# Attention blocks in pairs, and TensorE in source order, in a fused attention and expert kernel

## Chip, cores, metric

One Trainium2 chip, one of its cores. The metric is the device time of one execution in microseconds (us), lower is better. PE is TensorE, DVE is VectorE, ACT is ScalarE, POOL is GpSimd, SP the engine whose queue issues most of the DMAs.

## What is computed

Windowed attention, a dense layer with a clipped square as activation, then a routed layer with eight experts, of which each token takes one:

```python
scores = where(0 <= i - j < 64, q @ k.T / sqrt(64), -1e9)      # 4 x 8 heads, 576 tokens, 64 wide
attn   = exp(scores - max); attn /= sum + 1e-9
x = (attn @ v).transpose(0, 2, 1, 3).reshape(2304, 512)
h = x @ w_in                                                   # 512 x 2048
g = where(h >= 1, h, where(h <= -1, 0, (h + 1)**2 / 4))
x = g @ w_out                                                  # 2048 x 512
logits = x @ w_gate + modality_bias[modality_id]               # 8 experts
out[token] = gate * (relu(x @ w1[e]) @ w2[e]),  e = argmax(logits)
```

## The kernel before

The 2304 tokens are worked in six chunks of 384 (`NC`, `CT`). An attention block is 64 tokens with their eight heads, so a chunk has six blocks (`BPC`). While the dense layer runs for chunk c, the attention blocks of chunk c+1 are put between its steps. A chunk has 16 steps, f = 0 to 15, one for each 128 columns of the hidden layer. In a step PE does the first layer for f (`l1`, L435) and the second layer for f-2 (`l2`, L469, with `LAG` = 2). From chunk 1 on both layers work on a high and a low part of each operand (`gh` and `gl` from `gsplit`, L459): 12 matmuls for the first layer, and nine for the second, three for each of its three token tiles, the third of these on the low part. In chunk 0 both layers run in plain fp32, and DVE and ACT decode the weights beside that, one pair of tiles in a step (`dec_abs` on ACT, `dec_clamp` and `dec_merge` on DVE).

An attention block passes through five stages. `att_mm` (L321) makes scores on PE, `att_max` (L335) masks them and takes the maxima on DVE, `att_exp` (L350) takes exponentials and row sums on ACT. `att_norm` (L361) inverts the sums on DVE and scales, on ACT for the blocks of chunk 1 and on POOL later. `att_tr` (L380) transposes on PE, with a copy on ACT. `att_pv` (L393) multiplies by v in 16 matmul instructions of 64 output columns, two for each of the eight heads, and `att_x` (L412) copies the result out on ACT and leaves its low part on DVE. Scores, transposes, products with v and the rank products of the router share three PSUM banks (`aux`, L93).

Before, a new block starts at every second step. In chunk 0 (`step0`, L951) block number BPC + k starts at step `FIRST[k]`, is normalised one step later, transposed three and multiplied by v four steps later. In chunks 1 to 4 the loop over `its` (L995) starts it at `S0[k]`, transposes two and multiplies four steps later.

Who orders the instructions: in chunk 0 PE, DVE, ACT and POOL run in the order in which the source issues them (`manual_schedule`, `m0`). With chunk 1 this ends (`m0.close()`, L1005), and a planner with a model of the engines' times orders each engine's queue anew, except SP, which is in source order throughout. PE comes back to source order in the last part (L1075). A queue, once ordered, runs strictly in that order: what stands behind a waiting instruction waits too.

From step 1 of a chunk on the router of the chunk before runs as a generator (`route`, L514), one piece a step: it copies the second layer's results, makes the logits on DVE (L536), a one-hot of the chosen expert (L556), and at step 9 the rank products on PE (L561 and L563), in the source between the first and the second layer of that step.

Of the kernel before, what the change touches and what calls it, by code (L numbers as in the profile page):

```python
# [70 lines left out]
def moe_kernel(ctx, tc, qT, kT, v, w_in, w_out, mod, wg, wgT, mbias, w1, w2, cst, tri, empty, out, spec):  # L71
# [289 lines left out]
    def att_norm(i):  # L361
        att_sum(i)
        att_scale(i)
# [28 lines left out]

    def att_pv(i):  # L393
        ts = at.pop(i)
        vt = vs.pop(i)
        w = window(i)[0]
        if i < BPC:
            xo = ps.tile([P, KD, BLK], F32, name=f"xo{i}", tag="h", bufs=2)
        else:
            xo = aux([P, KD, BLK], f"xo{i}")  # L400
        for hp in range(KD):
            for a in range(2):
                T.matmul(
                    xo[a * D : (a + 1) * D, hp, :],
                    vt[:w, (2 * hp + a) * D : (2 * hp + a + 1) * D],
                    ts[:w, hp, a * BLK : (a + 1) * BLK],
                    start=True,
                    stop=True,
                )
        xos[i] = xo  # L410

    def att_x(i):  # L412
        xo = xos.pop(i)
        c, n = divmod(i, BPC)
        dst = slice(n * BLK, (n + 1) * BLK)
        if c == 0:
            A.copy(xs[c][:, :, dst], xo)
            return
        xh, xl = xs[c]
        A.copy(xh[:, :, dst], xo)  # L420
        V.tensor_tensor(xl[:, :, dst], xo, xh[:, :, dst].bitcast(F32), op=ALU.subtract)
# [517 lines left out]
    LAG = 2  # L939
    S0 = (0, 2, 4, 6, 8, 10)  # L940
    TRO, PVO = 2, 4
    def att_loads(i):
        if i % GB == 0 and i + GB < NB:
            load_k(i // GB + 1)
        load_v(i)
        if i + 2 < NB:
            load_q(i + 2)

    FIRST = (1, 3, 5, 7, 9, 11)

    def step0(f):  # L951
# [5 lines left out]
        if f >= NF - 2:  # L957
            split(2 if f < NF - 1 else 6)
        at_step = {f - st: BPC + k for k, st in enumerate(FIRST)}
        if 4 in at_step:  # L960
            att_pv(at_step[4])
            att_x(at_step[4])
        if 3 in at_step:
            att_tr(at_step[3])
        if 0 in at_step:
            att_mm(at_step[0])
            att_loads(at_step[0])
        l1(0, f)
        if f >= 4:
            act2(0, f - 1)  # L970
        dec_abs(f + 2)
        if 1 in at_step:
            att_norm(at_step[1])
        if 0 in at_step:
            att_max(at_step[0])
            att_exp(at_step[0])
        if f >= LAG:
# [10 lines left out]

    m2 = ExitStack()
    its = [(c, f) for c in range(NC) for f in range(NF)]  # L990
# [4 lines left out]
    for n in range(len(its) + LAG):  # L995
# [8 lines left out]
        if n == NF:  # L1004
            m0.close()  # L1005
        if n == len(its) - 1:
            m2.enter_context(tc.manual_schedule(engines={ET.Activation}))
        if n >= 1 and n - 1 < len(its):
            act2(*its[n - 1])
            gsplit(*its[n - 1])  # L1010
        if nxt is not None:
            for k, st in enumerate(S0):
                i = b0 + k
                if f == st + TRO:
                    att_tr(i)
            for k, st in enumerate(S0):
                i = b0 + k
                if f == st:
                    att_mm(i)
            for k, st in enumerate(S0):  # L1020
                i = b0 + k
                if f == st + PVO:
                    att_pv(i)
                    att_x(i)
                if f == st + 1:
                    att_norm(i)
            for k, st in enumerate(S0):
                i = b0 + k
                if f == st:
                    att_max(i)  # L1030
                    att_loads(i)
                    att_exp(i)
        if c == 1:
# [117 lines left out]
```

## Time and profile before

| | us |
|---|---|
| median of 3 runs | 747.73 (744.97 to 749.3) |
| profiled execution | 745.43 |
| its span, first to last instruction | 743.7 |
| PE busy in it | 731.2 |
| DVE busy | 497.2 |
| ACT busy | 417.1 |
| POOL busy | 145.5 |

How to read it: the span is what the trace covers, and the time of the execution has 1.7 us more around it. Busy is the time in which an engine has an instruction at work; matmuls overlap, so a busy PE can still issue more densely. A line such as L445 names the line of the kernel that issued the instruction.

### The profile page before, as it was taken

The page shows a single profiled execution, that of the slowest core. Times are in us where ns is not written, and L with a number is a line of the kernel's source. Part 1 is how long each engine was busy: PE and PEld are TensorE (multiplying, and loading weights), DVE is VectorE, ACT ScalarE, POOL GpSimd, SP SyncE. Part 2 cuts the span into 40 slices and gives each one's busy share as a digit, 9 for nine tenths or more (in the row PEclk, how much of TensorE's full clock was granted, in tenths as well). Part 3 has the DMA queues.
Part 4 walks back from the last instruction along what each step waited for, and adds up shares of the span by engine and source line. Part 5 has one row for each costly group of instructions (what it writes and reads, how often), then busy time and mean ns, then how long its engine had stood idle before and what let it go on. Part 6 is the DMA issues. An engine that isn't in the chain of part 4 may idle for free. (4 is left out here: it accounts for less than half of the span.)

```text
span 743.7 us, 13351 instructions
## 1 busy us (share of the span) xinstructions
PE 731.2 (98%) x4456; PEld 623.2 (84%) x4456; DVE 497.2 (67%) x1479; ACT 417.1 (56%) x981; POOL 145.5 (20%) x219
## 2 busy tenths in 40 slices
PE   8999999999999999999999999999999999999995
PEld 5655557888999899888998899899888988999884
DVE  5998889984396538752696468857776565755530
ACT  6775679555555545554555445546546555655531
POOL 3200002112011200120110252061266342221110
PEclk9999999999999999999999999999999999999998
DMA  9886633123032203121310014147768667666520
GB/s 323 323 307 221 245 124 99 61 80 57 29 107 79 65 29 106 45 79 15 106 58 30 1 59 156 58 72 233 249 161 265 220 231 246 222 206 209 196 91 19
DMA packets 55774, 101.89 MB, mean 137 GB/s; under 512 B 8032, under 2 KB 17376, under 8 KB 55568
## 3 DMA queue, kind: packets, MB, share of 16 engines
q1 hardware_dynamic: 50976, 90.92, 37.4%
q0 software_dynamic: 4576, 9.79, 4.4%
q8 instruction: 37, 0.61, 0.3%
q14 instruction: 41, 0.34, 0.1%
q10 hardware_dynamic: 144, 0.24, 0.1%
HBM read 91.46 MB, written 9.84 MB: 136 GB/s over the span
## 5 line engine op out<-in xcount | busy, mean ns | idle before, releaser
L445 PE MATMUL h<-xh,w 128*128 128x384 f32 x640 | 180.4, 342 | 0.0
L483 PE MATMUL py<-w,gh 128*128 128x512 f32 x480 | 149.2, 394 | 0.0
L728 DVE TENSOR_TENSOR e<-wr,e 128x512 fp32r<-128x512 f32 x160 | 106.8, 688 | 47.0 <-ACT e L727 42.7
L727 ACT CAST e<-wr 128x512 fp32r<-128x512 f32 x160 | 96.9, 619 | 66.5 <-DMA wr<-in_w 65.1
L445 PEld LDWEIGHTS h<-xh,w 128*128 128x128 f32 x640 | 117.0, 188 | 4.5 <-DVE u L457 0.8
L814 PE MATMUL yo<-e,hm 128*128 128x512 f32 x456 | 112.0, 397 | 1.2 <-DVE hm L800 0.7
L448 ACT ACTIVATE u<-h,half 128x384 f32<-128x384 f32 x96 | 55.7, 580 | 99.0 <-PE h L445 74.9
L445 PE MATMUL h<-xl,w 128*128 128x384 f32 x320 | 108.0, 337 | 0.0
L791 PE MATMUL hp<-zh,e 128*128 128x256 f32 x576 | 106.5, 284 | 0.0
L814 PEld LDWEIGHTS yo<-e,hm 128*128 128x128 f32 x456 | 83.7, 188 | 20.5 <-DVE hm L800 1.6
L483 PEld LDWEIGHTS py<-w,gh 128*128 128x128 f32 x480 | 88.8, 188 | 13.9
L457 DVE SCALAR_TENSOR_TENSOR u<-u,h 128x384 f32<-128x384 f32 x80 | 44.2, 552 | 74.9 <-ACT u L449 69.2
L483 PE MATMUL py<-w,gl 128*128 128x512 f32 x240 | 93.1, 393 | 0.0
L791 PEld LDWEIGHTS hp<-zh,e 128*128 128x128 f32 x576 | 90.3, 190 | 0.6
L536 DVE CUSTOM_DVE_ANT_0 prod<-y,wgb 128x512 f32<-128x512 f32 x120 | 85.2, 710 | 0.9
L791 PE MATMUL hp<-zl,e 128*128 128x256 f32 x288 | 81.5, 283 | 0.0
L465 ACT CAST gh<-u 128x384 fp32r<-128x384 f32 x80 | 41.0, 512 | 61.6 <-PE py L483 33.3
L378 POOL TENSOR_TENSOR s<-s,sm 128x512 f32<-128x512 f32 (+1 forms) x24 | 26.9, 1120 | 239.5 <-DVE sm L368 93.9
L466 DVE TENSOR_TENSOR gl<-u,gh 128x384 fp32r<-128x384 f32 x80 | 45.3, 566 | 25.9 <-ACT gh L465 19.3
L445 PEld LDWEIGHTS h<-xl,w 128*128 128x128 f32 x320 | 60.2, 188 | 2.6 <-issue 0.2
L791 PEld LDWEIGHTS hp<-zl,e 128*128 128x128 f32 x288 | 54.8, 190 | 0.5
L355 ACT ACTIVATE s<-s,mx 128x128 f32<-128x128 f32 (+1 forms) x120 | 46.2, 388 | 15.3 <-DVE mx L345 15.3
(206 smaller groups left out, 1024.4 us busy)
## 6 DMA issues: line engine op xcount, KB each, us to landing
wr<-in_w SPq DMA_DIRECT2D x160, 256.0 KB
q<-in_qT SPq DMA_DIRECT2D x32, 256.0 KB
dec<-in_w_in SPq DMA_DIRECT2D x16, 512.0 KB
dec<-in_w_out SPq DMA_DIRECT2D x16, 512.0 KB
v<-in_v SPq DMA_DIRECT2D x27, 256.0 KB
k<-in_kT SPq DMA_DIRECT2D x15, 384.0 KB
yd<-y SPq DMA_DIRECT2D x18, 256.0 KB
wgb<-in_wgT SPq DMA_DIRECT2D x1, 2048.0 KB
```

The lines of the kernel that those rows point to most:

```text
L355: A.activation(s[:, hp, :n], s[:, hp, :n], AF.Exp, bias=mx[:, hp : hp + 1], scale=-1.0, accum_out=sm[:, hp : hp + 1],)
L445: T.matmul(h, wi(f, a)[:, k, :], b[:, k, :], start=n == 0, stop=n == 3 * KD - 1)
L448: A.activation(u, h, AF.Relu, bias=half, scale=0.5)
L457: V.scalar_tensor_tensor(g, u, 1.0, h, op0=ALU.min, op1=ALU.max)
L465: A.copy(gh, u)
L466: V.tensor_tensor(gl, u, gh.bitcast(F32), op=ALU.subtract)
L483: T.matmul(ys[c][t], a[:, sl], wo(f, b), start=f == 0 and n == 0, stop=f == NF - 1 and n == 2)
L536: V.tensor_tensor_reduce(prod, yt[t], wgb[0][:, e, :], 1.0, 0.0, ALU.mult, ALU.add, lg[:, t, e : e + 1])
L727: A.copy(wpart(i, p, 0), t)
L728: V.tensor_tensor(wpart(i, p, 1), t, wpart(i, p, 0).bitcast(F32), op=ALU.subtract)
L791: T.matmul(hp[:, u, :], w1s(i, 2 * fp + u, k, a), b[:, k, :], start=n == 0, stop=n == 3 * KD - 1,)
L814: T.matmul(yo, a[:, f, sl], w2s(i, f, b), start=n == 0, stop=n == 3 * NF2 - 1)
```

## The change

Three things. From the second chunk's blocks on, blocks go in pairs: a pair starts at every fourth step (`FIRST` and `S0` now have three starts), both blocks' scores stand together in the first step, both transposes together three steps later, both products with v together four steps later, into one PSUM tile of 512 columns that is copied out at once. Maxima and exponentials of the first block are in the pair's first step and those of the second in the next; each is normalised one step after. Loads of v and q for both blocks are issued in the pair's first step. And PE is in source order from chunk 1 to the step before the last of chunk 5.

```diff
     def att_pv(i):
+        if i < BPC:
+            xo, o = ps.tile([P, KD, BLK], F32, name=f"xo{i}", tag="h", bufs=2), 0
+        else:
+            o = i % GB
+            xo = xos[i - 1] if o else aux([P, KD, GT], f"xo{i}")
         ts = at.pop(i)
         vt = vs.pop(i)
         w = window(i)[0]
-        if i < BPC:
-            xo = ps.tile([P, KD, BLK], F32, name=f"xo{i}", tag="h", bufs=2)
-        else:
-            xo = aux([P, KD, BLK], f"xo{i}")
         for hp in range(KD):
             for a in range(2):
                 T.matmul(
-                    xo[a * D : (a + 1) * D, hp, :],
+                    xo[a * D : (a + 1) * D, hp, o * BLK : (o + 1) * BLK],
...
     def att_x(i):
         xo = xos.pop(i)
         c, n = divmod(i, BPC)
-        dst = slice(n * BLK, (n + 1) * BLK)
         if c == 0:
-            A.copy(xs[c][:, :, dst], xo)
+            A.copy(xs[c][:, :, n * BLK : (n + 1) * BLK], xo)
             return
+        xos.pop(i + 1)
+        dst = slice(n * BLK, n * BLK + GT)
         xh, xl = xs[c]
         A.copy(xh[:, :, dst], xo)
         V.tensor_tensor(xl[:, :, dst], xo, xh[:, :, dst].bitcast(F32), op=ALU.subtract)
...
-    S0 = (0, 2, 4, 6, 8, 10)
-    TRO, PVO = 2, 4
     def att_loads(i):
-        if i % GB == 0 and i + GB < NB:
+        if i + GB < NB:
             load_k(i // GB + 1)
-        load_v(i)
-        if i + 2 < NB:
-            load_q(i + 2)
-
-    FIRST = (1, 3, 5, 7, 9, 11)
+        for u in range(i, i + GB):
+            load_v(u)
+            if u + GB < NB:
+                load_q(u + GB)
+
+    def att_step(i, n, pe):
+        if n == 4 and pe:
+            for u in range(GB):
+                att_pv(i + u)
+            att_x(i)
+        if n == 3 and pe:
+            for u in range(GB):
+                att_tr(i + u)
+        if n == 0 and pe:
+            for u in range(GB):
+                att_mm(i + u)
+            att_loads(i)
+        if 1 <= n <= GB and not pe:
+            att_norm(i + n - 1)
+        if n < GB and not pe:
+            att_max(i + n)
+            att_exp(i + n)
+
+    S0, FIRST = (0, 4, 8), (1, 5, 9)
...
     def step0(f):
...
-        at_step = {f - st: BPC + k for k, st in enumerate(FIRST)}
-        if 4 in at_step:
-            att_pv(at_step[4])
-            att_x(at_step[4])
-        if 3 in at_step:
-            att_tr(at_step[3])
-        if 0 in at_step:
-            att_mm(at_step[0])
-            att_loads(at_step[0])
+        todo = sorted([(st - f, BPC + GB * k) for k, st in enumerate(FIRST) if f >= st])
+        for n, i in todo:
+            att_step(i, -n, True)
         l1(0, f)
         if f >= 4:
             act2(0, f - 1)
         dec_abs(f + 2)
-        if 1 in at_step:
-            att_norm(at_step[1])
-        if 0 in at_step:
-            att_max(at_step[0])
-            att_exp(at_step[0])
+        for n, i in todo:
+            att_step(i, -n, False)
...
         if n == NF:
             m0.close()
+            m1.enter_context(tc.manual_schedule(engines={ET.PE}))
         if n == len(its) - 1:
+            m1.close()
             m2.enter_context(tc.manual_schedule(engines={ET.Activation}))
...
         if nxt is not None:
-            for k, st in enumerate(S0):
...
+            todo = sorted([(st - f, b0 + GB * k) for k, st in enumerate(S0) if f >= st])
+            for pe in (True, False):
+                for o, i in todo:
+                    att_step(i, -o, pe)
```

## Rows read from the trace of the kernel before

**Rows 1.** The page's first part: busy us of each engine, share, instructions.
```profile
PE 731.2 (98%) x4456; PEld 623.2 (84%) x4456; DVE 497.2 (67%) x1479; ACT 417.1 (56%) x981; POOL 145.5 (20%) x219
```

**Rows 2.** Busy table by stretches: PE, PEld, DVE, ACT, POOL, clock, DMA share, GB/s.
```profile
34.00:46.00 12.00, 12.00 (x55) 6.61 (x54) 11.96 (x34) 9.68 (x25) 0.00 (x0) 1.00 0.96 351
...
113.30:130.00 16.70, 16.70 (x82) 13.26 (x81) 16.25 (x43) 15.88 (x37) 2.35 (x9) 1.00 0.26 78
```

**Rows 3.** Timeline of PE, chunk 1: start us, length, line, operation, tiles, count.
```profile
184.22 0.39 PE L483 MATMUL py<-w,gl 128*128 128x512 f32 x1
184.53 0.69 PE L403 MATMUL xo<-ts,v 128*64 128x64 f32 x16
...
187.37 0.62 PE L483 MATMUL py<-w,gh 128*128 128x512 f32 x2
...
189.43 0.34 PE L445 MATMUL h<-xh,w 128*128 128x384 f32 x1
...
193.60 0.67 PE L330 MATMUL sc<-k,q 128*128 128x64 f32 x5
```

**Rows 4.** Line L403 in that stretch: least, median and greatest ns of one.
```profile
L403 PE MATMUL xo<-ts,v x16: 222/222/271, 184.5 to 185.0; 128*64 128x64 f32 x16
```

**Rows 5.** Timeline of PE, chunk 0, steps 3 to 6.
```profile
39.58 0.60 PE L385 MATMUL pt<-cs,s 128*128 128x128 f32 x4
40.02 2.75 PE L428 MATMUL h<-x,raw 128*128 128x384 f32 x8
42.60 2.74 PE L475 MATMUL py<-raw,g 128*128 128x512 f32 x6
...
55.05 2.74 PE L475 MATMUL py<-raw,g 128*128 128x512 f32 x6
```

**Rows 6.** Timeline of DVE, chunk 0, steps 3 and 4.
```profile
37.10 0.53 DVE L457 SCALAR_TENSOR_TENSOR g<-u,h 128x384 f32<-128x384 f32 x1
...
41.30 0.28 DVE L345 CUSTOM_DVE_ANT_0 s<-sc,cs 128x128 f32<-128x128 f32 x1
...
42.14 0.75 DVE L265 TENSOR_SCALAR dt<-dt 128x512 f32<-128x512 f32 x2
...
46.35 0.16 DVE L367 TENSOR_SCALAR sm<-sm 128x4 f32<-128x4 f32 x1
46.55 0.18 DVE L368 RECIPROCAL sm<-sm 128x4 f32<-128x4 f32 x1
```

**Rows 7.** Timeline of ACT, chunk 0: the scaling of block 6.
```profile
37.22 1.28 ACT L376 ACTIVATE s<-s,sm 128x128 f32<-128x128 f32 x4 [1.21 <-DVE sm L368]
```

**Rows 8.** Timeline of DVE, chunk 0: start and end of one decoding.
```profile
56.98 0.99 DVE L265 TENSOR_SCALAR dt<-dt 128x512 f32<-128x512 f32 x2 [0.39 <-ACT dt L258]
...
60.97 0.41 DVE L421 TENSOR_TENSOR xl<-xo,xh 128x256 fp32r<-128x256 f32 x1
```

**Rows 9.** Timeline of PE, chunk 1, second layer of step 2.
```profile
126.10 1.65 PE L483 MATMUL py<-w,gh 128*128 128x512 f32 x6
...
129.80 0.85 PE L483 MATMUL py<-w,gl 128*128 128x512 f32 x3
```

**Rows 10.** Timeline of DVE there: the low part for that second layer.
```profile
127.48 0.54 DVE L466 TENSOR_TENSOR gl<-u,gh 128x384 fp32r<-128x384 f32 x1
```

**Rows 11.** Timelines of PE and DVE, chunk 5, step 9 and the router's one-hot.
```profile
473.11 0.62 PE L483 MATMUL py<-w,gh 128*128 128x512 f32 x2
...
474.47 0.18 DVE L556 TENSOR_TENSOR oh<-cs,mf 128x24 f16<-128x24 f32 x1
```

**Rows 12.** The span's end by stretches, and two groups of equal matmuls (busy, mean ns).
```profile
735.80:739.50 3.70, 0.00 (x0) 0.00 (x0) 0.00 (x0) 0.69 (x1) 0.98 (x1) 1.00 0.18 66
739.50:743.70 4.20, 0.00 (x0) 0.00 (x0) 0.00 (x0) 0.00 (x0) 0.00 (x0) 0.50 0.01 4
...
L883 PE MATMUL warm<-wz 128*128 128x512 f16 x10 | 4.4, 631 | 1.3 <-DVE wz L880 1.3
...
L891 PE MATMUL idle<-wz 128*128 128x512 f16 x6 | 1.8, 384 | 0.0
```

More of the change, by code (lines that the diff above doesn't have):

```diff
@@ L987, in step0 @@
             )
-    m2 = ExitStack()
+    m1, m2 = ExitStack(), ExitStack()
     its = [(c, f) for c in range(NC) for f in range(NF)]
@@ L1011, in moe_kernel @@
         if nxt is not None:
-            for k, st in enumerate(S0):
[L1013 to L1032, printed above, removed]
+            todo = sorted([(st - f, b0 + GB * k) for k, st in enumerate(S0) if f >= st])
+            for pe in (True, False):
+                for o, i in todo:
+                    att_step(i, -o, pe)
         if c == 1:
```

## The prediction

> **What bounds the kernel now.** I read the page's first part first: TensorE (PE) is busy for 98% of the span, VectorE (DVE) for 67% [rows 1]. On such a page an engine that is only "busy on average" can still set the end of a stage, so I read the busy table by stretches next. In a stretch of chunk 0 and in the first steps of chunk 1 the share of DVE is 11.96 of 12.00 and 16.25 of 16.70 us, while PE is full in both [rows 2]. The reader is to see two things there: PE is the bound everywhere, so a microsecond saved on PE is a microsecond of the run, and in these two stretches DVE is full beside it, so a PE that asks earlier for something that comes through DVE will wait. Then I read PE's own timeline, group by group, for what a group of products with v costs, and the timelines of DVE and ScalarE (ACT) at the places where the new order makes PE ask earlier.
>
> **Part 1, products with v in one group: a gain.** A step of two layers without attention takes 193.60 - 189.43 = 4.17 us. Nine products of the second layer take 189.43 - 187.37 = 2.06, so 0.23 each. The last of them before a group of products with v starts at 184.22; without the group the next step would start at 184.45 and end at 188.62, and it ends at 189.43 [rows 3]. So one group of 16 costs 0.81 us. The 16 matmuls themselves last 0.69 us from first start to last end, and one lasts 0.22 [rows 3, 4], so the starts lie within 0.47 us and 16 of them are worth 0.50. The other 0.31 us is the passage from matmuls of 128 output columns to 64 and back. Two blocks in one group pay it once: 15 pairs (three for each of chunks 1 to 5) by 0.31 gives **-4.7 us**, all on PE, the engine that sets the end. Bounds: nothing, if a group of 32 breaks up, and 0.35 each, 5.2 in all. Scores and transposes stay as many as before and keep their kind; no row shows a passage that their pairing would save, so I put nothing there.
>
> The copy of the product is now one of 512 columns on ACT and one subtraction on DVE in place of two of 256. It lies beside PE work, and I cost it at nothing; if DVE's cover is gone, it is a few tenths in our favour.
>
> **Part 2, chunk 0: the second block's chain has one step less before its transposes.** Here all four engines run in source order before and after. Before, a block's row sums are normalised one step after its scores and its transposes come three steps after. Now the second block of a pair has its maximum in step 1, its normalising in step 2 and its transposes in step 3, so the normalising lies at the end of DVE's step just ahead of PE's request. DVE runs late here. For blocks 6 and 7 (steps f=1 to 4):
> PE is unchanged up to the end of step 3, since the scores of block 7 only move from f=3 to f=1. It reaches the transposes at 39.58, does those of block 6 until 40.02 [rows 5], and asks for those of block 7.
> DVE reaches the activation of step 3 at 37.10 now. The maxima of block 7 take 42.14 - 41.30 = 0.84 and move ahead of this point. From 37.10 to 41.30 it needs 4.20 for that activation and the decoding of one pair of weight tiles. So it is at the two small normalising operations at 37.10 + 0.84 + 4.20 = 42.14, and these take 46.73 - 46.35 = 0.38: 42.52 [rows 6]. ACT scales four heads in 1.28 [rows 7]: 43.8 us, and with some hundredths for signals 43.9.
> PE so waits 43.9 - 40.0 = **3.9 us**. Queued behind the waiting transposes on PE are the first layer of step 4 and all that follows. ACT's relu of step 4 waits for that layer, and ACT's absolute values of the next weights, behind the relu, so DVE does not use the pause to get ahead.
>
> For the other two pairs the same step by step. From the end of the first layer of step 5, ACT's relu, square and absolute values take until DVE starts decoding, as 56.98 - 55.05 = 1.93 [rows 5, 8]. Then DVE needs 3.99 (60.97 - 56.98) for decoding, some 1.7 for activation, normalising and maxima, 3.8 for the next decoding, 0.9 for activation and normalising, and ACT 1.3 for scaling: 13.6. PE is at the second block's transposes after one second layer, two steps of 2.58 (42.60 - 40.02) and 2.6, and one set of transposes (0.44): 13.4 [rows 5, 6, 8]. That is 0.2 to 0.3 us each, between 0 and 1. **Chunk 0 waits 4.4 us** (3.5 to 6).
>
> The loads: a pair now issues both v and both q in its first step, so 0.5 MB go on SP's queue two steps earlier, past one decode load (1 MB). At the 351 GB/s of that stretch [rows 2] this load lands 1.5 us later. What hides it is that DVE is a step behind and will be 0.8 us later still; if that cover were gone it would cost up to 1.5. The second q load waits for the second block's scores, which now stand in the same step, so SP is not held. POOL has no attention work in chunk 0.
>
> **Part 3, PE in source order in chunks 1 to 5: what the planner had moved.** In chunks 2 to 4 the planner's order is nearly the source's, so I cost this at nothing; what covers it is that the operands come a step early, and that POOL, which scales these blocks, is busy for 20% of the span [rows 1]. If that cover is gone, it is a wait of tenths at each of 12 pairs. Two places differ.
> Chunk 1, step 2: the planner ran the six matmuls on the high part (126.10), then the next first layer, and took the low part only at 129.80 [rows 9]. The low part was ready at 127.48 + 0.54 = 128.02 [rows 10]. In source order PE asks for it after two matmuls (0.46), with no transposes before it and with the scores of the second block (0.8) moved to the start of the chunk: at about 126.1, so a wait of 1.9 us. For it to be longer: that second block's scores came after the first layer of step 2 before, so its maxima and exponentials lay behind the low part; now they are ready ahead of it (0.8 on DVE, more on ACT), and its transposes, one step later, may wait too. For it to be shorter: the waits in chunk 0 hold PE back and not all of DVE. No row shows the new order of DVE, so the bounds are 0 and 6; I take **2.5 us**, near the row.
> Chunk 5, step 9: the rank products stand behind the first layer that ends at 473.11; their one-hot operand was finished at 474.47 + 0.18 = 474.65 [rows 11]. The planner had put them a step later. In source order PE waits **1.5 us** (0 to 2), with the second layer queued behind.
>
> **Sum:** -4.7 + 4.4 + 2.5 + 1.5 = +3.7 us. The profiled execution took 745.43 us (span 743.7), so 749.1 by its own measure. The median of the runs shown is 2.3 us above that execution, which lies near the fastest of them; carried to the median the forecast is 751.4.
>
> **The rivals.**
> (a) Source order costs nothing outside chunk 0, because the planner, told of PE's order, puts the low part and the one-hot ahead on DVE. Then -4.7 + 4.4 = -0.3: 747.4 at the median, not slower. For it: both late operands were behind work on DVE that could have waited. Against: DVE is full in the first of the two places [rows 2]. It decides from the point at which the low part is ready by 126.1.
> (b) The first steps of chunk 1 fall apart: low part and transposes both wait, 6 in place of 2.5: +7.2, 754.9. For it: DVE has 0.45 us free in 16.7 there [rows 2].
> (c) The clock. At the end of the span PE has no matmul from 735.8 on; the granted clock is 1.00 until 739.5 and 0.50 (the lower level, 1.2 GHz) after that [rows 12]. The pause of 3.9 us in chunk 0 is as long as this. At the start of the span ten matmuls of one shape took 0.63 us each, 4.4 us in all, that take 0.38 later [rows 12]; if a slow stretch after the pause is as long and runs at half speed, it loses 2.1 to 2.2: +5.8, 753.5. The Trainium skill ("TensorE: Matmul & The Clock Gate", section "Why this matters for your kernels") says that an idle stretch between bursts of matmuls puts the clock back to half; by that rule this rival holds, and the row at the end of the span agrees with it, while no row shows it inside the span.
> (d) The pairing does not save the passage, because 32 matmuls into one bank do not run through: +8.4, 756.1.
> (e) All waits stay out, the first too, if DVE's normalising of block 7 is done by 38.6: -4.7, 743.0. Only an error in my reading of DVE's order could bring this.
>
> **How the numbers follow.** Forecast 0.47, (a) 0.24, (b) 0.12, (c) 0.09, (d) 0.03, (e) 0.05. The predicted time is that of the forecast, 751.4. From (a) less 1.4 to (b) plus 1, with the unknown costs inside, the range is 746 to 756; it leaves (d), (e) and the tails out. A measurement of this kernel tells 0.5%, some 3.7 us, from no change; the forecast lies on that line. Its own half above the line with (b), (c), (d) gives slower 0.47, (e) with a little of (a) faster 0.07, and 0.46 is left for the same.
>
> **What would show it.** Right: in the trace after, groups of 32 products with v and steps shorter by some 0.3 us per pair in chunks 2 to 4; a PE gap of about 3.9 us at 40 us ahead of the second block's transposes, released by ACT's scaling, and two small ones some 25 us apart; a PE wait on the low part near the first second layer of chunk 1; the rank products of chunk 5 right behind the first layer after a gap of 1.5. Wrong: no gap at 40 us, since then chunk 0 gains; gaps in chunks 2 to 4, since then source order costs where I put nothing; a granted clock below 1 after the gap.

## The result, and the profile after

After: **751.77 us** (median of 11 runs, 748.89 to 753.35). Before, timed beside it on the same chip: 747.03 us (11 runs, 743.35 to 749.3). The ratio is **1.0066**, with a 95% interval of 1.0046 to 1.0086: slower by 0.7%. The middle of the interval is over the 0.5% that the prediction called its line, its lower end is not. The profiled execution of after took 751.95 us, its span is 750.3.

PE does almost the same work, as the page's first part shows beside [rows 1]. The page's clock row, the span in 40 slices of 18.8 us, has an 8 in its seventh slice, at the seam of chunks 0 and 1.

```profile
PE 732.9 (98%) x4456; PEld 624.8 (83%) x4456; DVE 499.6 (67%) x1464; ACT 414.9 (55%) x966; POOL 149.0 (20%) x219
...
PEclk9999998999999999999999999999999999999999
```

The list of PE's waits in after (total us, times, longest) puts two places ahead of all others; before had neither.

```profile
PE h L447 <- DVE g L459: 3.1, 1, 3.1
PE pt L385 <- ACT s L376: 2.8, 1, 2.8
```

**Chunk 0.** PE's timeline of after answers [rows 5]. The second block's transposes begin at 42.84, after a wait of 2.81 us for the scaling on ACT, and the first layer of step 4 at 43.88 instead of 40.02. That layer then takes 48.16 - 43.88 = 4.28 us instead of 2.58.

```profile
39.43 0.60 PE L385 MATMUL pt<-cs,s 128*128 128x128 f32 x4
42.84 1.20 PE L385 MATMUL pt<-cs,s 128*128 128x128 f32 x4 [2.81 <-ACT s L376]
43.88 4.44 PE L430 MATMUL h<-x,raw 128*128 128x384 f32 x8
48.16 1.02 PE L477 MATMUL py<-raw,g 128*128 128x512 f32 x2
```

The busy table of after by stretches (columns as in [rows 2]) says why: PE is busy throughout the first stretch and its granted clock is at half (0.51). The second stretch belongs to the seam, below; in the stretch behind it, 133 to 140, the clock is 1.00.

```profile
44.20:47.70 3.50, 3.50 (x7) 1.94 (x6) 2.34 (x5) 0.47 (x1) 0.00 (x0) 0.51 0.77 252
...
126.00:133.00 7.00, 5.88 (x15) 4.84 (x16) 6.35 (x12) 4.61 (x10) 0.00 (x0) 0.51 0.00 0
```

**The seam of chunks 0 and 1.** PE's timeline there: the second place is not the low part of [rows 9, 10]. The first layer of step 1 of chunk 1 waits 3.08 us for a PSUM bank `h`. There are two; this one is free when DVE has clamped the hidden tile of chunk 0's last step (`act2(0, 15)`, L459). Then the clock is at half again, until 133, and 131.13 - 127.12 = 4.01 us go for the twelve matmuls of a first layer, which take 2.11 at full clock (the median of later steps).

```profile
121.31 2.74 PE L477 MATMUL py<-raw,g 128*128 128x512 f32 x6
127.12 0.69 PE L447 MATMUL h<-xh,w 128*128 128x384 f32 x1 [3.08 <-DVE g L459]
...
131.13 3.68 PE L477 MATMUL py<-dt,g 128*128 128x512 f32 x6
```

Followed back: that clamp ran on DVE at 126.53, and it needs the square (L451) of the same tile from ACT. ACT's timeline shows the relu of step 15 at 118.62 and its square only at 123.95, with eight copies for the split of chunk 1's weights (L301) between. They take 4.95 us, where the eight at 112.42 took 4.24, since they keep pace with eight one-column copies on POOL (`hold_back`, L292) that keep the weights' places until the clamp of step 14. In before, relu and square of step 15 stood at 110.82 and 111.80, with one such copy between them and ten behind. The rows of ACT, then POOL's and DVE's, and ACT's in before:

```profile
112.42 4.24 ACT L301 CAST w<-raw 128x512 fp32r<-128x512 f32 x8
...
118.62 0.57 ACT L450 ACTIVATE u<-h,half 128x384 f32<-128x384 f32 x1
119.10 4.95 ACT L301 CAST w<-raw 128x512 fp32r<-128x512 f32 x8
123.95 0.52 ACT L451 ACTIVATE u<-u 128x384 f32<-128x384 f32 x1
...
119.06 4.93 POOL L292 COPY hold<-g 128x1 f32<-128x1 f32 x8 [4.33 <-DVE g L459]
...
126.53 0.54 DVE L459 SCALAR_TENSOR_TENSOR g<-u,h 128x384 f32<-128x384 f32 x1
```

```profile
110.82 0.58 ACT L448 ACTIVATE u<-h,half 128x384 f32<-128x384 f32 x1
...
111.80 0.52 ACT L449 ACTIVATE u<-u 128x384 f32<-128x384 f32 x1
113.55 5.30 ACT L301 CAST w<-raw 128x512 fp32r<-128x512 f32 x10 [1.22 <-POOL hold L292]
```

One thing lies before that. In the source the first pair's scores for chunk 1 stand behind step 15, in step 0 of chunk 1. In after's queue all 16 stand ahead of the first layer of step 15 (113.97), 14 of them even ahead of that of step 14 (108.59). So PE does not run in source order across the seam, where one stretch of source order ends and the next begins, and the pair's eight exponentials run on ACT ahead of the relu of step 15. PE's timeline of after:

```profile
107.03 1.73 PE L330 MATMUL sc<-k,q 128*128 128x128 f32 x14
```

**Chunks 2 to 4.** PE's timeline of after: the products of a pair are one group of 32, where [rows 3] has one of 16 for each block. The first layer of step 15 starts at 278.32 in chunk 2 and at 357.37 in chunk 3: a period of 79.05 us. The same two points lay 79.84 apart before. The rows of after, then of before:

```profile
278.32 0.34 PE L447 MATMUL h<-xh,w 128*128 128x384 f32 x1
...
343.68 1.15 PE L404 MATMUL xo<-ts,v 128*64 128x64 f32 x32
...
357.37 0.34 PE L447 MATMUL h<-xh,w 128*128 128x384 f32 x1
```

```profile
269.34 0.34 PE L445 MATMUL h<-xh,w 128*128 128x384 f32 x1
...
349.18 0.34 PE L445 MATMUL h<-xh,w 128*128 128x384 f32 x1
```

**Stage by stage.** I took the start of the first layer of step 15 in each chunk, and of the expert slots 1 and 3, from the traces of before and after, and subtracted. Chunk 0 lost 5.94 us (some 1.0 of it is work that moved up from chunk 1: 16 scores stand ahead of the mark in place of 6), chunk 1 lost 3.87, chunks 2, 3 and 4 gained 0.83, 0.79 and 0.99, chunk 5 lost 0.87, and the expert slots 1 and 2 gained 1.46. The sum, 6.6 us, is the difference of the spans (750.3 - 743.7).

### The profile page after: what moved, and what is told of

It is laid out like the page before. It is cut to its first block, busy times and chain, and to the rows that moved or that the text cites. A ratio compares the mean times of both kernels' runs of the same rounds, so it can differ in the third digit from the quotient of the medians.

```text
span 750.3 us, 13320 instructions
## 1 busy us (share of the span) xinstructions
PE 732.9 (98%) x4456; PEld 624.8 (83%) x4456; DVE 499.6 (67%) x1464; ACT 414.9 (55%) x966; POOL 149.0 (20%) x219
## 5 line engine op out<-in xcount | busy, mean ns | idle before, releaser
L459 DVE SCALAR_TENSOR_TENSOR u<-u,h 128x384 f32<-128x384 f32 x80 | 44.1, 552 | 72.2 <-ACT u L451 69.7
```

The lines of the kernel that those rows point to most:

```text
L459: V.scalar_tensor_tensor(g, u, 1.0, h, op0=ALU.min, op1=ALU.max)
```

## Experiments

Each was timed beside before on the same chip, but e1 to e4 and e9 to e11, then e5 to e8, then e12 ran on three different chips. So between these groups it is the ratio that compares, and not the median. The table has the median, the ratio to before with its interval, and the same stages as above: the loss against the trace of before, in us, from one profiled execution each.

| run | us | ratio (95%) | chunk 0 | chunk 1 | chunks 2-4 | chunk 5 | slots 1-2 |
|---|---|---|---|---|---|---|---|
| after | 751.77 | 1.0066 (1.0046-1.0086) | 5.94 | 3.87 | -2.61 | 0.87 | -1.46 |
| e1 source order only | 749.88 | 1.0036 (1.0021-1.0052) | -0.29 | 1.82 | -0.03 | 0.73 | 1.93 |
| e2 pairs, planned | 752.32 | 1.0071 (1.0049-1.0092) | 5.67 | -0.30 | -2.55 | 0.02 | 2.66 |
| e3 chunk 0 mended | 747.57 | 0.9999 (0.9980-1.0017) | -0.38 | 4.28 | -2.61 | 0.67 | 1.24 |
| e4 pause filled | 752.06 | 1.0063 (1.0044-1.0083) | 4.33 | 1.96 | -2.61 | 0.41 | -0.60 |
| e5 = e2 + e3 | 748.23 | 1.0011 (0.9992-1.0030) | -0.33 | 2.99 | -2.55 | 0.02 | 3.87 |
| e6 = e3, two groups | 750.93 | 1.0051 (1.0033-1.0069) | -0.12 | 5.64 | 0.22 | 0.67 | -0.76 |
| e7 = e3, chunk 1 later | **743.95** | 0.9955 (0.9938-0.9971) | -1.98 | 0.56 | -2.61 | 0.42 | 1.34 |
| e8 = e3, chunk 1 planned | 747.41 | 0.9996 (0.9982-1.0011) | 0.00 | 3.09 | -2.61 | 1.04 | 1.55 |
| e9 = e7, planned | 748.71 | 1.0008 (0.9990-1.0026) | -0.19 | 3.63 | -2.55 | 0.02 | 1.73 |
| e10 = after, chunk 1 later | 750.24 | 1.0038 (1.0017-1.0058) | 3.65 | 1.85 | -2.61 | 0.47 | 0.72 |
| e11 singly, chunk 1 later (undone) | 747.51 | 0.9996 (0.9977-1.0015) | -0.37 | -0.08 | 0.12 | 0.00 | 2.89 |
| e12 = e3, ACT's order | 748.42 | 1.0007 (0.9992-1.0023) | -2.34 | 5.22 | -2.61 | 0.99 | 1.68 |

The column of chunk 0 is 1.6 to 2.3 us lower, and that of chunk 1 higher, where the first pair's scores for chunk 1 stand behind step 15 (e7, e10, e12). The last column moves by 5 us although no edit touches the code of these slots; more on it below.

### Source order alone (e1)

```diff
         if n == NF:
             m0.close()
+            m1.enter_context(tc.manual_schedule(engines={ET.PE}))
         if n == len(its) - 1:
+            m1.close()
```

in the kernel before, blocks singly.

> Before, with TensorE in source order over chunks 1 to 5 and nothing else: single blocks, products with v block by block. Chunk 0 is untouched. Theory one (the wait of chunk 1 in the changed kernel comes from pairing and source order together, because the second block's exponentials and maxima stand ahead of the last activation of chunk 0): only the rank products of chunk 5 (0.8 to 1.5 us) and a small wait in chunk 1 (0 to 2 us) remain, so 1 to 3 us slower than before. Rival (source order alone makes the whole wait of chunk 1, some 5 us with the clock): 5 to 6.5 us slower.

Slower by 0.36%, some 2.6 us, as theory one had it. Chunks 2 to 4 are as before to 0.03 us; chunk 1 loses 1.8, and chunk 5 loses 0.7 at the rank products. In the profiled execution the slots lose 1.9 more, with a wait of 1.86 us and a granted clock of 0.50 from 553.56 to 556.97. The largest wait in chunk 1 on PE's timeline of e1 is for POOL's scaling of a block:

```profile
123.91 0.66 PE L385 MATMUL pt<-cs,s 128*128 128x128 f32 x4 [1.30 <-POOL s L378]
```

### Pairs alone (e2)

```diff
-            m1.enter_context(tc.manual_schedule(engines={ET.PE}))
...
-            m1.close()
```

in the changed kernel.

> The changed kernel, with TensorE left to the planner from chunk 1 on. Chunk 0 keeps its pause at the second block's transposes. Theory one (source order costs the changed kernel some 5 us at the start of chunk 1 and 0.8 in chunk 5): 1 us faster to 2 us slower than before, 4 to 6 us faster than the changed kernel. Rival (the wait in chunk 1 comes from pairing alone, since the last activation of chunk 0 is late on VectorE and ScalarE whatever the order of TensorE): 4 to 5 us slower than before, as the changed kernel.

Theory one expected a gain of 4 to 6 us, and there is none: 752.32 (six runs). The rival's number came out, 5 us slower than before, but not by its reason. Chunk 0 is untouched by this edit. Chunk 1 and chunk 5 improve by 4.2 and 0.85 us in the trace as expected, but the slots after them lose 2.66 where after's trace has gained 1.46. The square of step 15 is late in e2 too (relu 118.35, square 123.69), but the planned PE has other work there and waits 1.10 us. So source order is not what makes the changed kernel slow.

### The order of chunk 0 (e3)

```diff
+        d = int(i < 2 * BPC)
-        if n == 4 and pe:
+        if n == 4 + d and pe:
...
-        if n == 3 and pe:
+        if pe:
             for u in range(GB):
-                att_tr(i + u)
+                if n == 3 + d * u:
+                    att_tr(i + u)
```

In chunk 0 the second block's transposes, and the pair's products, come one step later.

> The changed kernel, with the transposes of the second block of each pair of chunk 0 one step later and the pair's products with v one step later too. Theory one (the pause at 40 us is the normalising of the second block, which comes out of VectorE a step too late): the gap and the two small ones vanish, the clock stays at full, chunk 0 ends 5 to 6 us earlier; 5 us faster than the changed kernel, level with before within 2 us if chunk 1 keeps its wait. Rival (VectorE is late in chunk 0 anyway, and the wait comes up elsewhere, at the products or at the first layer): less than 2 us faster than the changed kernel.

Theory one held: 747.57, the ratio falls from 1.0066 to 0.9999, some 5 us. The wait and the half clock behind it are gone together; step 4's first layer starts at 39.41 and takes 41.99 - 39.41 = 2.58 (PE's timeline of e3).

```profile
39.41 2.75 PE L430 MATMUL h<-x,raw 128*128 128x384 f32 x8
41.99 2.74 PE L477 MATMUL py<-raw,g 128*128 128x512 f32 x6
...
121.13 0.69 PE L447 MATMUL h<-xh,w 128*128 128x384 f32 x1 [3.48 <-DVE g L459]
```

The wait at the seam stays (last line), 3.48 us, with half clock behind it.

### The clock alone (e4)

```diff
             for u in range(GB):
+                if i + u == BPC + 1:
+                    fill = aux([P, KD, P], "fill")
+                    for _ in range(13):
+                        T.matmul(fill[:, 0, :], C["ident"], C["ident"], start=True, stop=True)
                 att_tr(i + u)
```

> The changed kernel, with 13 products of the identity by itself (26 matmul instructions, some 2.9 us, of which nothing reads the result) between the transposes of the two blocks of the first pair of chunk 0. They fill the pause and need nothing that is late. If the fall of the granted clock behind the pause costs what the slow first layer shows (4.28 in place of 2.58 us): the clock stays at full there, and the kernel is 1.5 to 2 us faster than the changed one. If the clock's fall only takes time that VectorE would have taken anyway: the same within 0.5 us, or slower by what the filler runs over the pause.

In the profiled execution the filler does what it should. The same layer, behind a pause of the same length but with PE at work in it, has the full clock and takes 2.6 us, and chunk 0 is 1.6 us shorter. PE's timeline of e4, and its busy table by stretches:

```profile
39.72 3.07 PE L960 MATMUL fill<-cs 128*128 128x128 f32 x26
42.94 1.21 PE L385 MATMUL pt<-cs,s 128*128 128x128 f32 x4 [0.15 <-ACT s L376]
43.98 2.75 PE L430 MATMUL h<-x,raw 128*128 128x384 f32 x8
```

```profile
43.00:48.00 5.00, 5.00 (x16) 2.76 (x17) 3.64 (x8) 2.97 (x8) 0.00 (x0) 1.00 0.74 262
```

The median is 752.06 all the same, not less than after's, so the 1.5 to 2 us that were expected did not come. The run that was profiled is the second shortest (748.79); the ten spread from 748.38 with a mean clock of 0.996 to 755.02 with 0.990. So the other runs of this kernel lose clock somewhere that this one trace doesn't show; after the seam's wait is likely, since e4 has that wait too (3.06 us, without a fall in this trace), but it is not shown.

### Pairs alone with the mended chunk 0 (e5), and source order from chunk 2 on (e8)

e5 is e3 with e2's edit. e8 is e3 with this:

```diff
         if n == NF:
             m0.close()
+        if n == 2 * NF:
             m1.enter_context(tc.manual_schedule(engines={ET.PE}))
```

> The changed kernel without the source order on TensorE (it is planned in chunks 1 to 5, as in the kernel before), and with the mended order in chunk 0 (transposes of a pair's second block and the pair's products one step later). Theory one: chunk 0 costs nothing any more (the run with pairs and a planned TensorE reached chunk 1 5.88 us late, the run with the mended order 0.92 us early), chunk 1 costs the 0.4 that the planned run showed, chunks 2 to 4 give 0.8 each, and there is no wait for the rank products. At the first slot that makes about 4 us less than before; the slots gave 2.8 us back in the planned run, which leaves 744 to 746.5, a ratio of 0.996 to 0.999. Rival: whatever is gained ahead of the slots is given back there in full, because the weights come as late as before: 747 to 748. Rival: the planner, with the first chunk shorter, runs into a chunk 1 as bad as that of the source order: 747.5 to 750.

> The run with the mended order in chunk 0, with TensorE planned in chunk 1 and in source order from chunk 2 on. Theory one: of the cost of chunk 1 (it ends 5.7 us later, by its distance to before, than it begins, in the run with the mended order) the fixed order of TensorE makes most, as a planned TensorE runs the second layer and other ready work where the fixed one waits; chunk 1 then costs 0.4 to 1.5 us, and the time is 743 to 745. The source order in chunks 2 to 5 alone then costs no more than the wait of 0.5 us for the rank products, against the run that is planned throughout. Rival: the wait in chunk 1 comes from the other engines' order, which is planned in both, and stays: 747 to 748.5.

748.23 and 747.41, against 747.57 with source order throughout: no difference that these intervals tell. In both the rival was right that chunk 1 keeps its wait. With PE planned the wait at the seam is still there, 2.6 us; the list of PE's waits in chunk 1 of e8 has nothing else:

```profile
PE h L447 <- DVE g L459: 2.6, 1, 2.6
```

e2's good chunk 1 (-0.30) goes with its late entry, 5.7 us, since e5 differs from e2 in chunk 0 alone. So the wait does not come from the fixed order of PE. The late square is there in both, 5.52 us behind its relu. In chunks 2 to 4 source order gives and takes 0.06 us.

### What a passage costs (e6)

Against e3:

```diff
         if n == 4 + d and pe:
-            for u in range(GB):
-                att_pv(i + u)
-            att_x(i)
+            att_pv(i)
+            if d:
+                att_pv(i + 1)
+                att_x(i)
...
             l1(c, f)
+        for o, i in todo if nxt is not None else ():
+            if o == -4:
+                att_pv(i + 1)
+                att_x(i)
```

> The run with the mended order in chunk 0, in which the products of a pair's second block, and the copies of the pair's output, stand behind the first layer of their step in chunks 1 to 4, so that the pair is two groups of eight 64 x 64 products again: 12 pairs, 24 groups in place of 12. All else is as in the run with the mended order (747.57 us). Theory one, that a group pays for its way in and out whatever its length: 12 x 0.31 = 3.7 us more, a period of chunks 2 to 4 of 79.8 to 79.9 us in place of 79.0, and a time of 750.7 to 751.5. Rival: the 0.25 to 0.3 us for each pair in the chunks' periods come from the fixed order of TensorE or from other engines, and not from the groups: periods stay at 79.0 and the time within 747 to 748.3.

Theory one: 750.93, 3.4 us over e3 by the medians and 3.9 by the ratios, so 0.28 to 0.32 for each of 12 pairs. Each pair is two groups of 16. On PE's timeline of e6 the period from chunk 2 to chunk 3 is 354.87 - 274.92 = 79.95 us, where the group of 32 gives 79.05: 0.30 for each of the three pairs.

```profile
274.92 0.34 PE L447 MATMUL h<-xh,w 128*128 128x384 f32 x1
...
354.87 0.34 PE L447 MATMUL h<-xh,w 128*128 128x384 f32 x1
```

### The start of the pairs in chunk 1 (e7, e9, e10, e11)

e7 is e3 with the pairs of chunk 1 two steps later:

```diff
-            todo = sorted([(st - f, b0 + GB * k) for k, st in enumerate(S0) if f >= st])
+            todo = sorted([(st + 2 * (c == 1) - f, b0 + GB * k) for k, st in enumerate(S0) if f >= st + 2 * (c == 1)])
```

> The run with the mended order in chunk 0, with the three pairs that are worked on in chunk 1 begun two steps later (steps 2, 6 and 10 in place of 0, 4 and 8). Theory one: the wait of 3.1 to 3.5 us ahead of the first layer of chunk 1's second step comes from the square and the clamp of the last step of chunk 0, which stand behind the weight splits and behind the masks and exponentials of the pair that starts just there; with the pair two steps later there is room for them, the wait is below 1 us, the granted clock doesn't fall, and chunk 1 ends 4 to 6 us earlier: 742 to 744.5. Rival: the splits alone hold the square and the clamp up, with the pair or without: the wait stays at 3 us and the time at 747 to 748. Rival: the pair's transposes, two steps later, meet the routing and the splits and make a wait of their own: the first wait goes, a second of 2 to 4 us comes at steps 5 to 7, 746 to 748.

743.95, ratio 0.9955: theory one, and the only version faster than before. ACT runs the square of step 15 at 110.37, ahead of the split copies, PE goes from step 0 to step 1 without a wait, and the clock is full throughout. In chunk 1 one wait of 0.72 us for a low part is left. The pair's scores stand behind step 15 here, at 120.55. The timelines of ACT and of PE in e7:

```profile
109.38 0.57 ACT L450 ACTIVATE u<-h,half 128x384 f32<-128x384 f32 x1
...
110.37 0.52 ACT L451 ACTIVATE u<-u 128x384 f32<-128x384 f32 x1
111.92 5.31 ACT L301 CAST w<-raw 128x512 fp32r<-128x512 f32 x10 [1.03 <-POOL hold L292]
```

```profile
115.49 0.74 PE L447 MATMUL h<-xh,w 128*128 128x384 f32 x1
...
120.55 1.95 PE L330 MATMUL sc<-k,q 128*128 128x128 f32 x16
...
125.80 0.50 PE L485 MATMUL py<-w,gl 128*128 128x512 f32 x1 [0.72 <-DVE gl L468]
```

e9 takes source order away from e7 (e2's edit).

> The run with both mends (chunk 0's order, and chunk 1's pairs two steps later; 743.95 us) with TensorE planned in chunks 1 to 5, without the source order. Theory one, by the runs with the mended chunk 0 (747.57 with source order throughout, 747.41 from chunk 2 on, 748.23 with none): the source order neither gives nor takes more than 0.5 us, 743.4 to 744.8. Rival: with the mends, the fixed order is what keeps TensorE's waits short in chunk 1 (one of 0.72 us is left there), and planned it loses 1 to 2 us: 745 to 746. Rival: the source order costs 1 to 3 us, as the run of it alone with single blocks did (749.88 against 747.31): 741 to 743.

A miss for all three theories: 748.71, with a ratio of 1.0008 for e7's 0.9955, so some 4 us more. The planner doesn't keep the later start. It puts the pair's scores back ahead of step 15, so seven of eight exponentials stand before the relu of step 15 and nine split copies before its square, and the wait at the seam is 2.89 us again. The timelines of ACT and of PE in e9:

```profile
112.09 0.56 ACT L450 ACTIVATE u<-h,half 128x384 f32<-128x384 f32 x1
...
112.94 4.77 ACT L301 CAST w<-raw 128x512 fp32r<-128x512 f32 x9
117.61 0.53 ACT L451 ACTIVATE u<-u 128x384 f32<-128x384 f32 x1
```

```profile
121.59 0.45 PE L447 MATMUL h<-xh,w 128*128 128x384 f32 x1 [2.89 <-DVE g L459]
```

So source order on PE is worth nothing by itself, and is needed for the later start to hold.

e10 is the changed kernel with the later start only, chunk 0 not mended.

> The changed kernel with chunk 1's pairs two steps later, and chunk 0 as the change has it. Theory one: the two costs are separate and add up: 751.8 less the 3.6 us that the later start gave in the run with chunk 0 mended, 747.5 to 749; the wait of 2.8 us at 42 us stays, that of 3.1 us at 127 us goes. Rival: the 2.8 us and the half clock of chunk 0 shift ACT's and POOL's work against TensorE so that chunk 1 has slack already, or the reverse: under 747 or over 750.

750.24, over the range of theory one and in the rival's: 1.5 us better than after by the medians and 2.1 by the ratios, where e7 was 3.6 and 3.3 better than e3. The wait in chunk 0 stays, 2.82 us. The wait at the seam is gone here too, and in its place PE's timeline has one of 1.93 us where the prediction had it, for the low part at the second layer of step 2:

```profile
132.72 0.50 PE L485 MATMUL py<-w,gl 128*128 128x512 f32 x1 [1.93 <-DVE gl L468]
```

The stages up to the slots add to 4.7 us less than after, and the slots lose 2.2 of that against after's trace. So by the medians the two costs don't simply add; why is open.

e11 is before with single blocks and chunk 1's starts one step later (1, 3, ..., 11).

> The kernel before, all blocks singly, with the blocks that are worked on in chunk 1 begun one step later (1, 3, ..., 11 in place of 0, 2, ..., 10). Theory one: the start in chunk 1 matters only for the pair's double share of masks and exponentials; the single block's share fits, as the profile of before has no wait of TensorE there, so nothing is gained: 746.5 to 748, and the 3.4 us by which the run with both mends beats before are the pairs'. Rival: the later start is worth the same with single blocks, by what it gives the weight splits, and pairs are not needed for it: 743.5 to 745.5.

747.51, ratio 0.9996: no gain, the number of theory one. But the trace of e11 shows that the later start did not take place. Its PE is planned, and its queue has the first block's eight scores where before has them: six at 106.89, ahead of the first layer of step 15 (107.66), and two at 112.82; relu and square of step 15 stand at 110.44 and 111.43 on ACT. As in e9, the planner undid the start. So the run does not answer its question. That the 3.4 us that e7 gains on before need the pairs is shown for the 2.61 us of chunks 2 to 4 alone; single blocks with source order and a later start in chunk 1 were not run.

### ACT's order at the seam (e12)

```diff
     m0 = ExitStack()
+    m1 = ExitStack()
+    m1.enter_context(tc.manual_schedule(engines={ET.PE, ET.Activation}))
-    m0.enter_context(tc.manual_schedule(engines={ET.PE, ET.DVE, ET.Activation, ET.Pool}))
+    m0.enter_context(tc.manual_schedule(engines={ET.DVE, ET.Pool}))
...
         if n == NF:
             m0.close()
+        if n == NF + 8:
+            m1.close()
             m1.enter_context(tc.manual_schedule(engines={ET.PE}))
```

in e3. The pair starts at step 0 as in the change. The edit was meant to alter ACT's order alone, but it alters PE's too: one stretch of source order now covers PE on both sides of the seam, and the pair's 16 scores, which e3 has at 105.87 ahead of step 15, stand behind it. PE's timeline of e12:

```profile
105.69 2.74 PE L430 MATMUL h<-x,raw 128*128 128x384 f32 x8
...
110.84 1.95 PE L330 MATMUL sc<-k,q 128*128 128x128 f32 x16
```

> The run with the mended order in chunk 0 (747.57 us), in which ScalarE too keeps source order through the first eight steps of chunk 1; the pair starts at step 0, as in the change. What this alters at the seam of the chunks: in the run it is built on, ScalarE's planned order puts the pair's eight exponentials and eleven weight casts of chunk 1 ahead of the square of chunk 0's last step, for which (over VectorE's clamp) the PSUM bank of chunk 1's second first layer waits; here that square stands right behind its relu. Theory one, that this order is what makes the wait of 3.5 us and the half clock behind it: the wait falls below 1 us and the time to 743.5 to 745.5, close to the run with the later start (743.95). Rival: it is the amount of ScalarE's and VectorE's work at the seam, and the fixed order only moves the wait, to the exponentials and so to the pair's transposes, or to the weights that the second layer needs: 747 to 750.

Both theories were right in part. With the square right behind its relu (108.47 and 109.08), the wait at the seam is gone and so is the fall of the clock. In after, e3 to e6, e8 and e9 the scores stand ahead of step 15, the square is 5.3 to 5.5 us behind its relu, and PE waits 2.6 to 3.8 us; in e7, e10 and e12 the scores stand behind, the square at most 1.0 us behind its relu, and there is no wait. So the late square is the cause of the wait. Whether ACT's fixed order or PE's brings the square forward, e12 cannot tell. With its edit four waits come at 147 to 165 us, 5.0 us together, and the time is 748.42; what makes them was not tested. ACT's timeline of e12, and PE's waits in its chunk 1:

```profile
108.47 0.58 ACT L450 ACTIVATE u<-h,half 128x384 f32<-128x384 f32 x1 [0.91 <-PE h L430]
109.08 0.52 ACT L451 ACTIVATE u<-u 128x384 f32<-128x384 f32 x1
```

```profile
PE h L447 <- DVE u L459: 3.1, 2, 2.1
PE xo L404 <- ACT ts L390: 1.3, 1, 1.3
PE pt L385 <- POOL s L378: 0.5, 1, 0.5
```

### The slots

No edit touches the expert slots, and yet slots 1 and 2 take from 1.46 us less to 3.87 more than in the trace of before. What PE waits for there is the relu of the hidden tile on ACT (`hm`), which stands behind copies of expert weights that wait for their DMA. Over 500 to 590 us ACT waited 29.6 us for these DMAs in before, 26.0 in after and 34.5 in e5 (groups by line of after, then of e5: busy, mean ns, idle before and its cause):

```profile
L729 ACT CAST e<-wr 128x512 fp32r<-128x512 f32 x57 | 34.4, 620 | 26.4 <-DMA wr<-in_w 26.0
```

```profile
L729 ACT CAST e<-wr 128x512 fp32r<-128x512 f32 x58 | 35.1, 619 | 35.0 <-DMA wr<-in_w 34.5
```

e11, which reaches slot 1 within 0.4 us of before and has its code from there on, loses 2.9 us more in them than before's trace. So the profile of before may be a good draw at this place. In e1 and e12 a granted clock of 0.50 for 3.41 us, from 553.6, is part of the loss. The three kernels that reach slot 1 four us or more after before (after, e4, e6) lose least, so a part of what is gained earlier may be given back here; what sets it stays open.

## Why the prediction came out right, point by point

The time, 751.4 for 751.77, and the side were right. Of the terms, one was right, and the others were off in both directions and partly cancelled.

- **Passages, -4.7.** Right where it can be read. Nine pairs in chunks 2 to 4 gave 2.61 us, 0.29 each, for the 0.31 of the sum, and e6 took the same back. Chunks 0 and 1 can't be read for it, since their waits cover it. Rival (d) is out.
- **Chunk 0, +4.4, of it 3.9 at the first pair.** The mechanism, its place and DVE's path are as worked out: DVE's small operations come at 41.98 (42.14 in the sum) and the pause is ahead of the second block's transposes, released by ACT. The wait is 2.81, because the transposes follow ACT's scaling head by head and don't wait for the fourth: the group lasts 1.04 us in place of 0.44. The sum took the scaling as one block of 1.28. Without a wait, the layer of step 4 would have begun two sets of transposes behind 39.43, at 40.31; it began at 43.88, so 3.57 were lost for the 3.9 of the sum. The other two pairs cost 0.2 and 0.4 us (groups of 1.04 and 1.29 us for 0.88), close to the 0.2 to 0.3 each.
- **Rival (c), the clock, 0.09.** It came true beside the forecast, at both places. In chunk 0 the layer behind the pause lost 1.7 us (4.28 for 2.58; the rival said 2.1 to 2.2). The prediction's own list has a granted clock below 1 after the gap among the signs of being wrong, and the sign is there. I set it against the forecast as if one excluded the other; it was a cost that the forecast's own wait brings along, and belonged into the sum with its chance. The Trainium skill ("TensorE: Matmul & The Clock Gate", section "Why this matters for your kernels") has the rule that an idle stretch between bursts puts the clock back to half; the rows inside the span now agree, 0.51 in both stretches, though in e4's trace a wait of 3.06 us was followed by no fall.
- **Chunk 1, +2.5 (0 to 6).** The step that failed: I looked for the late operand among what the pair itself and the second layer need, and put it at the low part. What came late was a bank, held by the last step of chunk 0, through ACT's order. In after the low part is not waited for. I had written that no row shows DVE's new order; it was ACT's that mattered. The sum had the second block's scores at the start of chunk 1, as the source has them; in after they run ahead of step 15, and the exponentials with them. The diff does not show this. The trace of before could have warned: six of its first block's eight scores stand ahead of step 15 too, at 107.26. Cost: 3.08 of wait and 1.89 in the first layer alone at half clock, more behind it; the chunk lost 3.87 and some 1.0 that the marks put into chunk 0, and three passages were gained (0.9 by the sum's price): 5.8 by the trace, inside the bounds and more than twice the 2.5. That the low part is a real candidate shows in e10, 1.93 for my 1.9, where the first wait is out of the way.
- **Source order outside these places, nothing.** Right in chunks 2 to 4 (e1, 0.03 us). In chunk 1 it costs 1.8 us with single blocks (e1), and with pairs 1.2 by the traces and nothing by the medians (e3 against e8).
- **Chunk 5, +1.5 (0 to 2).** Right in place, 0.68 in size; chunk 5 lost 0.87. The one-hot came earlier against PE than [rows 11] let me assume (PE's timeline of after):

```profile
481.18 0.19 PE L563 MATMUL rk<-oh,tri 128*128 128x32 f16 x1 [0.68 <-DVE oh L558]
```

- **The carry to the median.** I carried +3.7 from a profile 2.3 us under the median of its three runs, 747.73. Beside after, the median of before was 747.03, so the medians differ by 4.7 and not by 3.7: that the time came within 0.4 us is owed in part to a base that was 0.7 too high. The difference of the profiles is larger, 6.6 by the spans, since before's profile (745.43) stands 1.6 under that median and after's (751.95) 0.2 over its own.

So the sum by stages was 3.5 in chunk 0 (4.4 less three passages), 1.6 in chunk 1, -2.8, 1.5 and 0; measured, by the trace, 5.94, 3.87, -2.61, 0.87 and -1.46, or 4.9 in each of the first two with the scores put back into chunk 1. Two clock falls too little, a chunk 5 too dear, and slots that I had at nothing. A forecast that is right to 0.4 us in this way is right by luck in its second digit; its sign rests on chunk 0: with that mended, e3 has a ratio of 0.9999.

## What to carry to other kernels

When a regrouping saves a fixed price per group, look first at what the group makes the slower engines do at once: here 0.3 us per pair was won and 10 us lost at two places where masks and exponentials of two blocks met engines that were already full, and moving the work by one and by two steps there turned a loss of 0.7% into a gain of 0.45%. A wait of a few us on TensorE is to be costed together with the clock that it may lose. And a fixed order on one engine is worth what it keeps in place: taken alone it gave nothing, but without it the planner undid the later start, in e9 and in e11. Where one ordered stretch ends and the next begins, read the queue: here work crossed the seam. And read it in a control run as well, to see that the edit took place.

## What the runs showed of the hardware

- Of ten waits of 2.6 to 3.8 us on PE in these traces (after two; e2, e3, e5, e6, e8, e9 and e10 one; e4 one), nine were followed by a granted clock of 0.5, for 3.4 us in six cases and 6.8 in three. e4's, 3.06 us, was not. Of four waits of 1.9 to 2.1 us, three (e7, e10, e12) were not followed by one; e1's, 1.86 us in its slots with one of 0.48 close behind, was, for 3.4 us. Two of 1.39 and 0.49 close together in e12's slots were too, for 3.4 us, and two of 1.45 and 0.48 in e5's and of 1.67 and 0.48 in e2's were not.
- The runs of one kernel spread by 4 to 8 us where there are ten or more, and in most kernels the longer ones have the lower mean clock: e3 from 744.89 at 0.996 to 749.57 at 0.991, e7 from 740.93 at 0.998 to 747.17 at 0.993. Not in all: the longest run of after, 753.35, has 0.996, and that of e1, 752.51, has 0.998. A single profile can stand at either end.
- Eight one-column copies on POOL took 4.93 us in after, 2.56 in before and 1.01 in e12 for the same bytes. In after DVE ran subtractions of two tensors beside nearly all of them; in e12 it ran one clamp of 0.56 us beside them and no subtraction. That the two engines hinder each other there is my reading; no run tried it alone.
